# A Fourier mixing block on one core: the first batch's transposes on TensorE, its folds behind the inverse stage, and a new pacing of the seams

## The chip, the core and the metric

The kernel runs on one core of a Trainium2 chip. Its engines are TensorE (PE, matrix products into PSUM), VectorE (DVE), ScalarE (ACT), GpSimd (POOL) and SyncE (SP); here SP issues every DMA, from one queue, and 16 DMA engines carry them out. The metric is the device time of one execution in microseconds (us), the median of several runs.

## The reference

Eight batches of 3136 tokens with 256 channels go through a filter in the frequency domain, a two-dimensional Fourier mixing, and a channel MLP:

```python
X = np.fft.rfft(x, axis=1);  Y = X * (filt_r + 1j * filt_i)
x = np.fft.irfft(Y, n=3136, axis=1)
mixed = np.real(np.fft.fft(np.fft.fft(x, axis=1), axis=2))
u = x + mixed
un = (u - mean(u)) / sqrt(var(u) + 1e-6)          # over the 256 channels
out = u + maximum(un @ w_ch1, 0) @ w_ch2          # 256 -> 1024 -> 256
```

## The kernel before

All products are done in float16 with values split into a high and a low part, so most products come in three (high-high, high-low, low-high).

**Per batch, the way there** (`there`: `forward1`, or `first_forward1` for batch 0, then `forward2`). The 3136-point transform is split into 112 x 28. `forward1` loads x in seven tiles, finds the largest absolute value (`absmax`, DVE) for a power-of-two scale, does 14 pieces of the first stage (L386; L328 in batch 0) and writes each split piece `ast` to a DRAM buffer `d1`. `forward2` works in seven pieces `ch`: it loads `at` from `d1` (L411, which changes the layout), and for each of two channel halves `spectrum` does the second stage (L434 and L435), multiplies by the filters (DVE L440, L444; POOL L448, L449; in batch 0 some of this goes to DVE through `half`), splits the result into `y16` (ACT L453, then L454) and transposes `y16` into `z` with a transposing DMA (L459). `fold` (POOL L467 and L488, ACT L487) adds and subtracts the two channel halves and keeps the sums in the ring `eo`, from which the channel mixing is done later. `inverse1` (L495 to L497) does the first inverse stage two pieces behind, splits it into `bt` (ACT L499, DVE L500) and writes it to DRAM `d2`.

**The way back** (`inverse2`). It loads `b` from `d2` (L529), does the second inverse stage (L551), scales it on ACT (L558) and stores it in DRAM `dy`, in slots that hold a token and its mirror.

**Groups.** 12,544 slots are taken in 49 groups of 256. `fetch(g)` loads y, `prepare(g)` does the channel mixing from `eo` (L620), adds it (`add`, L630), normalizes (ACT L710), splits into `u16` (ACT L713, then DVE or POOL L715) and transposes into `ut` with a transposing DMA (L716). `first_product(g, f)` (L738) and `second_product(g, f)` (L767) are the MLP in eight f-steps a group; L776 adds and the result is stored.

**Weights** come as 64-bit floats in eight raw loads (`load_weights`, L810), are widened on DVE (`widen`, L787 to L793), bounded, scaled and split (`split_weights`, L850 to L852).

**What sets the order.** `there` and `back` are generators; one `yield` is one step. `advance(n)` runs steps of the way there, `give(n)` steps of the way back, and both are called from the main loop after every f-step `q` at a pace set by `RISE`, `EARLY`, `SOON`, `STEPS` and `BACK`; `bring` forces what a group needs. `weigh` issues work on the weights at given steps (`LOAD_AT`, `WIDEN_AT`, ...). Before the main loop batch 0 goes through all its steps, then groups 0 and 1 are prepared. A planner then orders each engine's instructions by its own estimates of time; `after(mark)` keeps an instruction behind the marked one on the same engine. `bufs` is how many buffers share a tag; the tag "big" (7 buffers) holds x, at, z and raw words, the tag "y" (4) holds the groups' y and widened weights.

Of the kernel before, what the change touches and what calls it, by code (L numbers as in the profile page):

```python
# [190 lines left out]
def _program(ctx, tc, nc, a, NB):  # L191
# [27 lines left out]
    s1 = cp.tile([112, 2, 112], F16, name="s1")  # L219
    s1f = cp.tile([112, 112], F32, name="s1f")  # L220
# [4 lines left out]
    ident = cp.tile([128, 128], F32, name="ident")  # L225
    ones = cp.tile([1, 128], F32, name="ones")
    eps = cp.tile([128, 1], F32, name="eps")
# [130 lines left out]
    def forward1(b, d1):  # L358
        xs = [xp.tile([112, 4, 256], F32, tag="big", name=f"x_{b}_{q}") for q in range(7)]
        m = tp.tile([112, 8], F32, tag="mx", name=f"mx_{b}")  # L360
        lag = 2 if b else 0
        for q in range(7 + lag):
            with after(("y", 1), ("un", 0)) if b == 1 else nullcontext():
                if q < 7:
                    nc.sync.dma_start(xs[q], a["x"][b, :, 4 * q : 4 * q + 4])
                if q >= lag:
                    with after("h"):
                        absmax(m[:, q - lag : q - lag + 1], xs[q - lag], AX.XY)
            if q < 7:
                yield  # L370
# [28 lines left out]
    def forward2(b, d1, d2):  # L399
# [21 lines left out]
        def spectrum(ch, hf):  # L421
            at = ats[ch]
            if hf == 0:
                yts[ch] = fp.tile([128, 2, 2, 4, 56], F32, tag="yt", name=f"yt_{b}_{ch}", bufs=2)
            yt = yts[ch]
# [21 lines left out]
            t2v = t2.rearrange("p r (j q) -> p r j q", j=4)  # L447
            half(b, hf == 1).tensor_tensor(yh[:, 0], yh[:, 0], t2v[:, 1], op=ALU.subtract)  # L448
            nc.gpsimd.tensor_tensor(yh[:, 1], yh[:, 1], t2v[:, 0], op=ALU.add)  # L449
# [7 lines left out]
            if hf == 0:  # L457
                zs[ch] = xp.tile([128, 8, 256], F16, tag="big", name=f"z_{b}_{ch}")
            marks["z", ch] = nc.sync.dma_start_transpose(  # L459
                zs[ch][:, :, 128 * hf : 128 * hf + 128], y16.rearrange("p j l q -> p (j l q)")  # L460
            ).ins

# [27 lines left out]
        def inverse1(ch, h):  # L490
            z = zs[ch][:112].rearrange("p (j l) c -> p j l c", l=2)[:, 2 * h : 2 * h + 2]
            j = 4 * ch + 2 * h
            p = bank(f"i1_{b}_{ch}_{h}")[:112].rearrange("p (j c) -> p j c", j=2)
            for i in range(2):
                nc.tensor.matmul(p[:, i], i1[:, j + i, 0], z[:, i, 0], start=True, stop=False)  # L495
                nc.tensor.matmul(p[:, i], i1[:, j + i, 0], z[:, i, 1], start=False, stop=False)  # L496
                nc.tensor.matmul(p[:, i], i1[:, j + i, 1], z[:, i, 0], start=False, stop=True)  # L497
            bt = fp.tile([112, 2, 2, 256], F16, tag="ast", name=f"bt_{b}_{ch}_{h}", bufs=4)
            nc.scalar.copy(bt[:, :, 0], p)  # L499
            nc.vector.tensor_tensor(bt[:, :, 1], p, bt[:, :, 0], op=ALU.subtract)  # L500
            nc.sync.dma_start(d2[:, j : j + 2], bt)

        far = 3
        for c in range(far):
            load(c)
        for _ in range(PAUSE):
            yield
        for c in range(9):
            work = [
                (c, spectrum, 0), (c, spectrum, 1), (c, fold, None), (c - 2, inverse1, 0), (c - 2, inverse1, 1),  # L510
            ]
            for ch, f, arg in work:
                if 0 <= ch < 7:
                    f(ch) if arg is None else f(ch, arg)
                    yield
            load(c + far)

    def inverse2(b, d2):
# [6 lines left out]
        def load(c):  # L525
            if c < 7:
                bts[c] = fp.tile([112, 4, 2, 256], F16, tag="b2", name=f"b2_{b}_{c}", bufs=2)
                with after("dy"):
                    marks["b", c] = nc.sync.dma_start(  # L529
                        bts[c].rearrange("p j h c -> p (j h) c"), d2v[:, 8 * c : 8 * c + 8]  # L530
                    ).ins

        def store(k, s, r, ys, c, j0):
            rows = dy[k, 224 * c : 224 * c + 224].rearrange("(j s q) c -> s q j c", j=4, s=2)
            marks["dy"] = nc.sync.dma_start(rows[s, :, j0], ys[r : r + 28, j0]).ins

        load(0)
        yield
        for c in range(14):
# [59 lines left out]
    def fetch(g):  # L599
        y = ys_of[g] = mp.tile([128, 2, 2, 256], F32, tag="y", name=f"y_{g}", bufs=4)  # L600
        for t, (g0, g1) in enumerate(groups[g]):
            q = g0
            while q < g1:
                b = q // NS
                e = min(g1, (b + 1) * NS)
                with after(("ut", 0)) if g == 2 else after(("out", g - 4)):
                    marks["y", g] = nc.sync.dma_start(
# [44 lines left out]
    def prepare(g):  # L652
# [52 lines left out]
        for t, (g0, g1) in enumerate(tiles):  # L705
# [9 lines left out]
            marks["u16", g] = low.tensor_tensor(u16[:m, :, :, 1], unv, u16[:m, :, :, 0], op=ALU.subtract).ins  # L715
            marks["ut", g] = nc.sync.dma_start_transpose(ut[:, t, :, :m], u16[:m].rearrange("p k d l q -> p (k d l q)")).ins  # L716
            yield
# [35 lines left out]
    def second_product(g, f):  # L753
# [8 lines left out]
        for t, (g0, g1) in enumerate(tiles):  # L762
# [12 lines left out]
            if f == 7:  # L775
                nc.vector.scalar_tensor_tensor(  # L776
                    y[:m, t], acc[:m], beta[:m], y[:m, t], op0=ALU.mult, op1=ALU.add
                )
                marks["out", g] = nc.sync.dma_start(a["out"][:, g0:g1].rearrange("k s c -> s k c"), y[:m, t]).ins

# [31 lines left out]
    def widen_weights(i):  # L812
# [54 lines left out]
    def advance(n):  # L867

        while done[0] < min(n, NB * STEPS):
            b, s = divmod(done[0], STEPS)  # L870
            if s in folds and b * NS + folds[s] - RING > mixed[0]:
                return
# [9 lines left out]
    folds = {20 + PAUSE + max(4 + 3 * ch, 5 * ch): 224 * ch + 224 for ch in range(7)}  # L882

    def need(slot):

        return BACK * (slot // NS) + 2 * (slot % NS // 224) + 3

    def bring(slot):
        advance(STEPS * (slot // NS + 1))
        give(need(slot))  # L890
# [47 lines left out]
    for q in range(8 * ng + LAG):  # L938
# [71 lines left out]
```

## Time and profile before

| | us |
|---|---|
| median of 3 runs | 1548.83 |
| range of the runs | 1542.42 to 1549.5 |
| profiled execution | 1553.5 |
| its span | 1551.7 |
| PE busy | 1403.2 (90% of the span) |
| DVE busy | 1095.7 (71%) |
| ACT busy | 757.2 (49%) |
| POOL busy | 535.7 (35%) |

Mean granted TensorE clock: 0.939 of full speed. The span runs from the first to the last instruction of one profiled execution; the profiled execution's own time is a little longer. A row of a group of instructions gives line, engine, operation, output from input, shapes and count, then busy us and mean ns of one, then the idle time before them and what ended it. A row of a timeline or of the chain gives start and duration in us. A row of the waits gives who waited for whom: us in total, times, longest. PE's durations in a row overlap (products are pipelined); the distance of their starts is what one costs.

### The profile page before, as it was taken

The numbers are of one execution on the slowest core, as the hardware profiler recorded it, in microseconds if no ns is written. First come the engines' busy times: TensorE is split into PE (matmuls) and PEld (weight loads), VectorE is DVE, ScalarE is ACT, GpSimd is POOL, SyncE is SP. The second block draws the span as 40 slices with busy tenths as digits, with TensorE's granted clock in tenths as the row PEclk, the third lists the DMA queues.
The fourth block names the chain that finished last, engine by engine and source line by source line (L and its number), as shares of the span: only waits on it lengthen the run. The fifth ranks groups of instructions, "written<-read, shape, count | busy, mean of one in ns | idle before, by whom it ended". The sixth has DMA issues, their size and how long they took to land.

```text
span 1551.7 us, 30099 instructions
## 1 busy us (share of the span) xinstructions
PE 1403.2 (90%) x11203; PEld 937.8 (60%) x11203; DVE 1095.7 (71%) x2395; ACT 757.2 (49%) x1409; POOL 535.7 (35%) x675
## 2 busy tenths in 40 slices
PE   5444998887999999999989899899999999999998
PEld 2431666554766667665766576665676666766666
DVE  5776877686768867786767777687857878565462
ACT  3256554364645545364535555364543755443431
POOL 3732038306710474006720175003740076110110
PEclk7565999998999999999999999999999999999999
DMA  8999269859983898559883799639994598644420
GB/s 251 221 277 254 67 157 204 192 168 207 214 230 98 229 217 219 135 151 216 202 213 83 192 211 206 187 107 200 219 220 122 165 223 192 170 110 122 106 52 31
DMA packets 446388, 273.17 MB, mean 176 GB/s; under 512 B 235521, under 2 KB 412721, under 8 KB 446241
## 3 DMA queue, kind: packets, MB, share of 16 engines
q1 hardware_dynamic: 446240, 271.25, 72.5%
q8 instruction: 88, 1.44, 0.4%
q14 instruction: 60, 0.48, 0.1%
HBM read 113.36 MB, written 102.76 MB: 139 GB/s over the span
## 4 chain that ended last, share of the span: by engine, by line
PE 67%; DMA 14%; DVE 8%; POOL 4%; issue 3%; ACT 2%; SPq 1%; DVEq 0%; ACTq 0%; POOLq 0%
PE h L738 27%; PE acc L767 26%; PE s L386 4%; PE y L551 3%; DMA d<-bt 3%; DMA at<-d 2%; PE mix L620 2%; DMA ut<-u 2%; DMA z<-y 2%; DMA d<-ast 2%; DMA x<-x 1%; DMA b<-d 1%; PE i L495 1%; DVE y L630 1%; PE i L496 1%
## 5 line engine op out<-in xcount | busy, mean ns | idle before, releaser
L738 PE MATMUL h<-ut,w1s 128*128 128x512 f16 x2352 | 594.4, 387 | 34.4 <-DMA ut<-u 28.9
L767 PE MATMUL acc<-w2s,h 128*128 128x256 f16 x4704 | 601.0, 274 | 3.9 <-ACT h L747 3.9
L767 PEld LDWEIGHTS <-h 128*128 128x128 f16 x4704 | 457.1, 98 | 152.5 <-issue 15.6
L748 DVE SCALAR_TENSOR_TENSOR h<-h,h 128x512 f16<-128x512 f32 x392 | 267.3, 684 | 238.2 <-ACT h L747 237.1
L747 ACT ACTIVATE h<-h 128x512 f16<-128x512 f32 x392 | 233.0, 594 | 369.9 <-PE h L738 363.6
L738 PEld LDWEIGHTS <-w1s 128*128 128x128 f16 x2352 | 225.3, 99 | 256.6 <-issue 44.4
L715 POOL TENSOR_TENSOR u<-un,u 128x512 f16<-128x512 f32 x94 | 107.8, 1163 | 730.1 <-ACT u L713 649.0
L630 DVE SCALAR_TENSOR_TENSOR y<-mix,alpha,y 128x508 f32<-128x508 f32 (+1 forms) x368 | 156.4, 474 | 10.2 <-DMA y<-dy 8.2
L558 ACT ACTIVATE ys<-y,alpha 128x512 f32<-128x512 f32 x112 | 75.8, 684 | 98.1 <-PE y L551 97.8
L710 ACT ACTIVATE un<-y,sb 128x256 f32<-128x256 f32 x196 | 101.7, 589 | 42.6 <-DVE sb L703 39.8
L454 POOL TENSOR_TENSOR y<-yt,y 128x448 f16<-128x448 f32 x105 | 108.5, 1037 | 28.5 <-ACT y L453 28.2
L551 PE MATMUL y<-b,i 112*64 112x512 f16 (+1 forms) x480 | 78.0, 419 | 37.4 <-DMA b<-d 28.3
L500 DVE TENSOR_TENSOR bt<-i,bt 112x512 f16<-112x512 f32 x112 | 75.7, 683 | 50.9 <-ACT bt L499 50.8
L448 POOL TENSOR_TENSOR yt<-yt,t 128x224 f32<-128x224 f32 x105 | 70.5, 671 | 115.3 <-DVE t L444 59.3
L440 DVE SCALAR_TENSOR_TENSOR yt<-s,pF,ft 128x448 f32<-128x448 f32 x112 | 75.6, 676 | 38.9 <-PE s L435 35.4
L499 ACT CAST bt<-i 112x512 f16<-112x512 f32 x112 | 65.0, 583 | 73.9 <-PE i L497 52.8
L453 ACT CAST y<-yt 128x448 f16<-128x448 f32 x112 | 62.5, 562 | 60.9 <-POOL yt L449 57.9
L776 DVE SCALAR_TENSOR_TENSOR y<-acc,beta,y 128x512 f32<-128x512 f32 x98 | 71.5, 745 | 23.8 <-PE acc L767 23.5
L434 PE MATMUL s<-s,at 112*128 112x56 f16 x896 | 65.5, 194 | 24.7 <-DMA at<-d 21.5
L495 PE MATMUL i<-z,i 112*112 112x256 f16 x224 | 64.7, 289 | 25.0 <-DMA z<-y 17.7
L386 PE MATMUL s<-x,s 112*112 112x512 f16 x294 | 85.9, 385 | 0.0
L389 DVE TENSOR_TENSOR ast<-s,ast 112x512 f16<-112x512 f32 x98 | 66.7, 681 | 24.0 <-ACT ast L388 23.7
(127 smaller groups left out, 1637.4 us busy)
## 6 DMA issues: line engine op xcount, KB each, us to landing
x<-x SPq DMA_DIRECT2D x56, 448.0 KB
d<-ast SPq DMA_DIRECT2D x112, 224.0 KB
at<-d SPq DMA_DIRECT2D x56, 448.0 KB
d<-bt SPq DMA_DIRECT2D x112, 224.0 KB
b<-d SPq DMA_DIRECT2D x56, 448.0 KB
out<-y SPq DMA_DIRECT2D x98, 256.0 KB
y<-dy SPq DMA_DIRECT2D x92, 256.0 KB
dy<-ys SPq DMA_DIRECT2D x208, 112.0 KB
```

The source lines that it names most:

```text
L386: nc.tensor.matmul(p, s1[:, hs], x16[:, hx], start=i == 0, stop=i == 2)
L454: last = half(b, hf == 1).tensor_tensor(ylo, ytv, yhi, op=ALU.subtract)
L495: nc.tensor.matmul(p[:, i], i1[:, j + i, 0], z[:, i, 0], start=True, stop=False)
L551: nc.tensor.matmul(p[64 * h : 64 * h + 64, js], i2[:, t, h, i], bt[:, o + js.start : o + js.stop, h], start=i == 0, stop=i == 1,)
L558: nc.scalar.activation(ys[:, o : o + 2], p, AF.Copy, scale=al[:, 2:3])
L630: nc.vector.scalar_tensor_tensor(out, p, al, y, op0=ALU.mult, op1=ALU.add)
L710: nc.scalar.activation(un[:m, k], y[:m, t, k], AF.Identity, bias=sb[:m, i, 1:2], scale=sb[:m, i, 3:4])
L715: marks["u16", g] = low.tensor_tensor(u16[:m, :, :, 1], unv, u16[:m, :, :, 0], op=ALU.subtract).ins
L738: marks["pe"] = nc.tensor.matmul(p[:, c0 : c0 + n].rearrange("p (t k q) -> p t k q", k=2, q=m), w1s[:, d, hw, 128 * f : 128 * f + 128], ut ...
L747: nc.scalar.activation(h[:, 0, :nt], p[:, :nt], AF.Relu)
L748: marks["h"] = nc.vector.scalar_tensor_tensor(h[:, 1, :nt], p[:, :nt], 0.0, h[:, 0, :nt], op0=ALU.max, op1=ALU.subtract).ins
L767: nc.tensor.matmul(acc[:m, k], h[:, hh, c0 : c0 + m], w2s[:, f, hw], start=f == 0 and k == 0 and i == 0, stop=f == 7 and k == 1 and i == 2,)
```

## The change

- `flip` transposes on TensorE: each 128-column block of a tile is transposed into one PSUM bank, and ACT copies the bank to its place. Batch 0 uses it for z in place of the transposing DMA (14 times), group 0 for ut (twice). A float16 identity `ident16` is made for it.
- In batch 0 the folds of pieces 2 to 6 are issued behind the last `inverse1`; their spectra are kept until then, four of them in the "y" buffers. In other batches a fold is issued after the inverse products of its step and one piece later. One subtraction of the second channel half in batch 0 (L448) goes from DVE to POOL.
- Four raw weight loads are issued during the last pieces of batch 0's first stage, four during its spectrum stage; widening stands behind the last `bt` subtraction.
- Pacing: absmax three steps behind its x load in place of two; x loads of batches from 2 on stand behind the last marked DMA; the three at loads are a step apart, and four steps lie between the first of them and the first spectrum, in place of two; two more empty steps between the first b load and its product; the way back is issued one step an f-step at most and begins 300 slots earlier; the last fold of a batch need not be done before its way back begins; `EARLY` is 0.6 in place of 0.54.

```diff
-PAUSE = 2
-STEPS = 22 + PAUSE + 7 * 5
-BACK = 15
-EARLY = 0.54
+PAUSE = 4
+XLAG = 3
+FIRST = 21 + XLAG
+STEPS = FIRST + PAUSE + 7 * 5
+WAIT = 2
+BACK = 1 + WAIT + 14
+EARLY = 0.6
+LOADED = 300
-LOAD_AT = (52, 52, 52, 52, 61, 61, 61, 61)
-LOAD_AFTER = (("z", 5), ("z", 5), ("z", 6), ("z", 6)) + (("b", 1),) * 4
-LOAD_IN = ('ut', 'ut', 'big', 'big', 'big', 'big', 'big', 'big')
-WIDEN_AT = (56, 57, 58, 59, 62, 63, 64, 65)
+LOAD_AT = (19, 20, 21, 22, 50, 50, 54, 54)
+LOAD_AFTER = (("d1", 10), ("d1", 11), ("d1", 12), ("d1", 13), ("bt", 3), ("bt", 3), ("bt", 4), ("bt", 4))
+LOAD_IN = ("ut", "ut", "ys", "ys", "big", "big", "big", "big")
+WIDEN_AT = (58, 59, 60, 61, 62, 63, 64, 65)
...
+    def flip(dst, src, pool, tag, name):
+        m, n, q = src.shape
+        pt = pool.tile([128, 8, 128], F16, tag=tag, name=name)
+        for i in range(n):
+            nc.tensor.transpose(pt[:q, i, :m], src[:, i], ident16[:m, :m])
+        return nc.scalar.copy(dst, pt[:q, :n, :m])
...
     # forward1
+                    with after("sp") if b > 1 else nullcontext():
+                        nc.sync.dma_start(xs[q], a["x"][b, :, 4 * q : 4 * q + 4])
...
     # spectrum
+                pool, tag, bufs = (mp, "y", 4) if b == 0 and 2 <= ch < 6 else (fp, "yt", 2)
...
-            half(b, hf == 1).tensor_tensor(yh[:, 0], yh[:, 0], t2v[:, 1], op=ALU.subtract)
+            nc.gpsimd.tensor_tensor(yh[:, 0], yh[:, 0], t2v[:, 1], op=ALU.subtract)
...
+            if b == 0:
+                marks["z", ch] = flip(
+                    z[:112], y16.rearrange("p j l q -> p (j l) q")[:, :, :112], ps_o, "pso", f"zt_{ch}_{hf}"
+                ).ins
+            else:
+                marks["z", ch] = nc.sync.dma_start_transpose(z, y16.rearrange("p j l q -> p (j l q)")).ins
...
     # forward2
         for c in range(far):
             load(c)
-        for _ in range(PAUSE):
+            if b:
+                yield
+        for _ in range(PAUSE - far if b else PAUSE + XLAG - 1):
             yield
...
-                (c, spectrum, 0), (c, spectrum, 1), (c, fold, None), (c - 2, inverse1, 0), (c - 2, inverse1, 1),
+                (c, spectrum, 0), (c, spectrum, 1), (c - 2, inverse1, 0), (c - 2, inverse1, 1),
+                (c - 1 if c < 7 else c - 2 if c == 8 else -1, fold, None),
...
-                if 0 <= ch < 7:
+                if 0 <= ch < 7 and (b or f is not fold or ch < 2):
...
+        for ch in range(2, 7) if b == 0 else ():
+            fold(ch)
+            yield
...
     # inverse2
         load(0)
-        yield
+        for _ in range(1 + WAIT):
+            yield
...
     # prepare
+            if g == 0:
+                ub = u16[:m].rearrange("p k d l q -> p (k d l) q")
+                flip(ut[:, t, :, :m], ub, ps_f, "psf", f"utt_{t}")
+            else:
...
     # widen_weights
-            with after("ylo" if "ylo" in marks else ("dve", 13)):
+            with after("low"):
...
     # give
-        while come[0] < min(n, NB * BACK) and done[0] >= STEPS * (come[0] // BACK + 1):
+        while come[0] < min(n, NB * BACK) and done[0] >= STEPS * (come[0] // BACK + 1) - 1:
...
+    def soon(slot):
+        return max(need(slot), BACK * ((slot + LOADED) // NS) + 1 + WAIT)
...
     # main loop
+        give(min(come[0] + 1, soon(32 * q + SOON)))
         advance(int(STEPS * (1 + min((q + 1) / RISE, (q + 1) / per + EARLY))))
-        give(BACK * (32 * q + SOON) // NS)
```

More of the change, by code (lines that the diff above doesn't have):

```diff
@@ L219, in _program @@
     s1 = cp.tile([112, 2, 112], F16, name="s1")
-    s1f = cp.tile([112, 112], F32, name="s1f")
+    s1f = fp.tile([112, 112], F32, tag="t2", name="s1f", bufs=2)
     s2 = cp.tile([112, 56, 2, 56], F16, name="s2")
@@ L225, in _program @@
     ident = cp.tile([128, 128], F32, name="ident")
+    ident16 = cp.tile([128, 128], F16, name="ident16")
     ones = cp.tile([1, 128], F32, name="ones")
@@ L235, in _program @@
     make_identity(nc, ident)
+    nc.scalar.copy(ident16, ident)
     nc.vector.memset(ones, 1.0)
@@ L360, in forward1 @@
         m = tp.tile([112, 8], F32, tag="mx", name=f"mx_{b}")
-        lag = 2 if b else 0
-        for q in range(7 + lag):
+        for q in range(7 + XLAG):
             with after(("y", 1), ("un", 0)) if b == 1 else nullcontext():
                 if q < 7:
-                    nc.sync.dma_start(xs[q], a["x"][b, :, 4 * q : 4 * q + 4])
-                if q >= lag:
+                    with after("sp") if b > 1 else nullcontext():
+                        nc.sync.dma_start(xs[q], a["x"][b, :, 4 * q : 4 * q + 4])
+                if q >= XLAG:
                     with after("h"):
-                        absmax(m[:, q - lag : q - lag + 1], xs[q - lag], AX.XY)
-            if q < 7:
+                        absmax(m[:, q - XLAG : q - XLAG + 1], xs[q - XLAG], AX.XY)
+            if q < 6 + XLAG:
                 yield
@@ L499, in inverse1 @@
             nc.scalar.copy(bt[:, :, 0], p)
-            nc.vector.tensor_tensor(bt[:, :, 1], p, bt[:, :, 0], op=ALU.subtract)
-            nc.sync.dma_start(d2[:, j : j + 2], bt)
+            marks["low"] = nc.vector.tensor_tensor(bt[:, :, 1], p, bt[:, :, 0], op=ALU.subtract).ins
+            marks["bt", ch] = nc.sync.dma_start(d2[:, j : j + 2], bt).ins
         far = 3
@@ L528, in load @@
                 with after("dy"):
[L529 removed]
+                    marks["b", c] = marks["sp"] = nc.sync.dma_start(
                         bts[c].rearrange("p j h c -> p (j h) c"), d2v[:, 8 * c : 8 * c + 8]
@@ L605, in fetch @@
                 e = min(g1, (b + 1) * NS)
-                with after(("ut", 0)) if g == 2 else after(("out", g - 4)):
+                with after(("un", 0)) if g == 2 else after(("out", g - 4)):
                     marks["y", g] = nc.sync.dma_start(
@@ L715, in prepare @@
             marks["u16", g] = low.tensor_tensor(u16[:m, :, :, 1], unv, u16[:m, :, :, 0], op=ALU.subtract).ins
-            marks["ut", g] = nc.sync.dma_start_transpose(ut[:, t, :, :m], u16[:m].rearrange("p k d l q -> p (k d l q)")).ins
+            if g == 0:
+                ub = u16[:m].rearrange("p k d l q -> p (k d l) q")
+                flip(ut[:, t, :, :m], ub, ps_f, "psf", f"utt_{t}")
+            else:
+                marks["sp"] = marks["ut", g] = nc.sync.dma_start_transpose(
+                    ut[:, t, :, :m], u16[:m].rearrange("p k d l q -> p (k d l q)")
+                ).ins
             yield
@@ L778, in second_product @@
                 )
-                marks["out", g] = nc.sync.dma_start(a["out"][:, g0:g1].rearrange("k s c -> s k c"), y[:m, t]).ins
+                marks["sp"] = marks["out", g] = nc.sync.dma_start(a["out"][:, g0:g1].rearrange("k s c -> s k c"), y[:m, t]).ins
     def widen(dst, raw, name):
@@ L870, in advance @@
             b, s = divmod(done[0], STEPS)
+            if s == 0 and come[0] < BACK * (b - 1) + 1:
+                return
             if s in folds and b * NS + folds[s] - RING > mixed[0]:
@@ L876, in give @@
     def give(n):
-        while come[0] < min(n, NB * BACK) and done[0] >= STEPS * (come[0] // BACK + 1):
+        while come[0] < min(n, NB * BACK) and done[0] >= STEPS * (come[0] // BACK + 1) - 1:
             next(home)
             come[0] += 1
-    folds = {20 + PAUSE + max(4 + 3 * ch, 5 * ch): 224 * ch + 224 for ch in range(7)}
+    folds = {FIRST + PAUSE + (4, 9, 14, 19, 24, 29, 34)[ch]: 224 * ch + 224 for ch in range(7)}
     def need(slot):
-        return BACK * (slot // NS) + 2 * (slot % NS // 224) + 3
+        return BACK * (slot // NS) + 1 + WAIT + 2 + 2 * (slot % NS // 224)
+    def soon(slot):
+        return max(need(slot), BACK * ((slot + LOADED) // NS) + 1 + WAIT)
     def bring(slot):
-        advance(STEPS * (slot // NS + 1))
+        advance(STEPS * (slot // NS + 1) - 1)
         give(need(slot))
```

14 lines of the change are left out of this document (6 added, 8 removed).

## The prediction

> **What bounds the kernel now.** I read the page first, then the span cut into stages, then 5 us slices of the first stage, the groups of instructions, the chain that ended last, and the waits of TensorE (PE). The stages (busy us of PE, PE weight loads, DVE, ACT, POOL with counts, granted clock, DMA share, GB/s):
>
> ```profile
> 0.00:149.80 149.80, 68.20 (x453) 43.16 (x453) 101.95 (x215) 68.17 (x132) 65.65 (x85) 0.62 0.93 252
> 149.80:400.00 250.20, 220.75 (x1796) 145.41 (x1797) 190.51 (x400) 125.54 (x233) 96.36 (x125) 0.94 0.74 170
> 400.00:1300.00 900.00, 867.12 (x7114) 581.89 (x7113) 669.46 (x1468) 465.90 (x867) 339.75 (x430) 0.98 0.78 185
> 1300.00:1551.70 251.70, 247.16 (x1844) 167.37 (x1842) 133.81 (x315) 97.61 (x179) 33.98 (x36) 1.00 0.41 103
> ```
>
> There are two programs in one. Up to 149.8 us, when the first product of the channel MLP starts, PE is busy 68.2 us and everything waits for batch 0 to come through. From then on PE is busy 1335.0 of 1401.9 us, so the end is set by PE's work plus its 66.9 us idle. Hence: time = start of the first product + 1335 + what PE idles. An edit counts if it moves the first product or removes PE idle time. The profiled execution took 1553.5 us (1.8 more than its span); the median of the runs is 1548.83, 4.7 lower. I work out differences in the span and take them off the median. About 0.5% (7.7 us) is what a measurement of this kernel can tell from no change.
>
> **Start-up, first half: the spectrum stage of batch 0 (45.7 to 102.5 us).**
>
> ```profile
> 25.00:30.00 5.00, 3.08 (x5) 0.93 (x4) 2.58 (x5) 4.97 (x11) 4.83 (x5) 0.50 0.58 201
> 35.00:40.00 5.00, 1.84 (x6) 0.55 (x4) 3.31 (x12) 2.70 (x7) 0.05 (x1) 1.00 0.51 155
> 55.00:60.00 5.00, 2.78 (x12) 2.40 (x12) 4.88 (x10) 2.37 (x5) 4.79 (x7) 0.50 0.94 231
> 65.00:70.00 5.00, 2.28 (x35) 1.74 (x33) 4.42 (x8) 2.08 (x4) 5.00 (x8) 0.50 1.21 266
> 70.00:75.00 5.00, 4.27 (x44) 4.10 (x44) 3.57 (x7) 2.23 (x5) 4.58 (x6) 0.50 1.13 323
> 45.71 0.23 PE L434 MATMUL s<-s,at 112*128 112x56 f16 x1 [6.11 <-DMA at<-d]
> 45.76 0.23 PE L435 MATMUL s<-s,at 112*128 112x56 f16 x1
> 81.41 0.25 PE L434 MATMUL s<-s,at 112*128 112x56 f16 x1
> L448 POOL TENSOR_TENSOR yt<-yt,t 128x224 f32<-128x224 f32 x105 | 70.5, 671 | 115.3 <-DVE t L444 59.3
> L467 POOL TENSOR_TENSOR ef<-yt 128x224 f32<-128x224 f32 x112 | 73.8, 677 | 0.8
> L488 POOL TENSOR_TENSOR eo<-ef,eo 128x448 f16<-128x448 f32 (+6 forms) x62 | 58.9, 953 | 35.4 <-ACT eo L487 34.7 <-DMA ut<-u 0.7
> L454 POOL TENSOR_TENSOR y<-yt,y 128x448 f16<-128x448 f32 x105 | 108.5, 1037 | 28.5 <-ACT y L453 28.2
> L453 ACT CAST y<-yt 128x448 f16<-128x448 f32 x112 | 62.5, 562 | 60.9 <-POOL yt L449 57.9
> L280 ACT ACTIVATE squares<-ft 128x784 bf16<-128x784 f32 x4 | 3.4, 849 | 0.0
> 56.85 0.43 PE L495 MATMUL i<-z,i 112*112 112x256 f16 x1 [3.58 <-DVE yt L440]
> 57.08 0.42 PE L496 MATMUL i<-z,i 112*112 112x256 f16 x1
> 111.10 1.37 PE L620 MATMUL mix<-mix,eo 128*128 128x129 f16 x13
> ```
>
> In the slices from 55 us the fifth busy number, POOL, is 4.6 to 5.0 of 5 us, and DMA's share is about 1: POOL sets the pace, DMA is full beside it. A piece (one of seven) costs POOL one L448 (0.67), two L449 (0.67 each, the same form as L448), one L454 (1.04), two L467 (0.68 each) and one L488 (0.95): 5.4 us; the measured period is (81.41 - 45.71)/6 = 5.95.
>
> *Folds moved back* (the "sums for the mixing"). Pieces 2 to 6 lose L467 x2 and L488 here, and gain the second L448, which goes from DVE to POOL: 4 x 0.67 + 1.04 = 3.7 us. POOL is no longer the bound. The five folds then run on POOL behind the last spectrum, about 4 us each with one buffer: 20 us. Their results are wanted by the second group only; the first group takes pieces 0 and 1, whose folds stay. Four of the "y" buffers hold the kept spectra, so the first fetch of y waits for fold 4, some 12 us behind the last spectrum; the fetch comes about 30 us behind it. Cost nothing, covered by the inverse stage.
>
> *z by TensorE.* Removed: 14 DMA transposes from SP's queue and the DMA engines. Added: 8 transposes of 112 or 128 columns and one ACT copy of 1024 columns for each half. A transpose streams 128 columns through PE; the nearest row is L620 at the same half clock, 1.37/13 = 0.105 us, so 0.84 us for eight. The ACT copy: L280 with 784 columns takes 0.849, L453 with 448 takes 0.562; the line through them gives 1.05 us at 1024. New loads per piece: ACT 2 x 0.56 + 2 x 0.58 + 2 x 1.05 = 4.4 (the 0.58 is L499 below); PE at half clock 32 x 0.047 (45.76 - 45.71) + 12 x 0.22 (57.08 - 56.85) + 1.7 = 5.8. So the period lies between 4.4 (ACT) and 5.95 (nothing won); I take 5.2, nearer PE's number, because the clock column stands at 0.50 in the three slices from 55 us, with PE up to 85% busy. 6 x 0.75 = 4.5 us. The Trainium skill (TensorE: Matmul & The Clock Gate, Part 1: The HAM clock gate) says that about 3.4 us of sustained work lifts PE from half to full clock; the slice 70 to 75, 4.27 us busy at 0.50, does not bear that out by itself. If it held here, ACT's 4.4 would be the period and the term 4.8 us larger.
>
> ```profile
> L499 ACT CAST bt<-i 112x512 f16<-112x512 f32 x112 | 65.0, 583 | 73.9 <-PE i L497 52.8 <-DMA d<-bt 12.1 <-issue 4.8
> L500 DVE TENSOR_TENSOR bt<-i,bt 112x512 f16<-112x512 f32 x112 | 75.7, 683 | 50.9 <-ACT bt L499 50.8
> 100.28 2.25 DMA d<-bt
> 102.69 0.92 SPq L529 DMA_DIRECT2D b<-d  x2
> 107.11 1.92 PE L551 MATMUL y<-b,i 112*64 112x256 f16 x12 [8.94 <-DMA b<-d]
> 104.31 6.87 DMA raw<-w
> 111.19 3.54 DMA dy<-ys
> 114.74 1.92 ACT w L850 x3
> 123.84 0.73 DVE y L630
> 135.37 2.08 ACT L710 ACTIVATE un<-y,sb 128x256 f32<-128x256 f32 x4 [0.81 <-DVE sb L703]
> 137.35 1.12 ACT L713 CAST u<-un 128x512 f16<-128x512 f32 x2
> 141.54 8.21 DMA ut<-u
> 149.80 0.61 PE h L738
> ```
>
> Tail of the stage: last spectrum at 81.41 to the last d2 landing at 102.53 is 21.1 us. After: products 1.5, four DVE steps 2.7 at most, POOL 1.3, ACT 0.6, DVE 0.8, flip 1.9, twelve inverse products 2.6, bt 1.3, landing 2.25, hand-overs 0.6: 15.5. Gain 5.6 us.
>
> *Weights loaded earlier.* Four of the eight raw loads (512 KB each) go in SP's queue behind the last four d1 writes, ahead of the first at load. 2.1 MB at the stage's 252 GB/s is 8.3 us of DMA in a place where the engines were half idle (share 0.58 and 0.51 in the first two slices); at can be late by 0 to 4 us, I take 2. So the first half wins 4.5 + 5.6 - 2 = 8.1 us.
>
> **Start-up, second half (102.5 to 149.8).** The chain shows four raw loads (6.87 us) between the loads of b and the dy stores, then weight scaling on ACT (1.92). All raws are now ahead of this stage. b's load (4.4 us from issue to the first product at 107.11) runs in part beside the raws, so of the 8.8 us I take 5. From 123.84 to 135.37 DVE works four widening instructions into the chain, some 0.5 each; they now stand behind the last bt subtraction and are mostly done: gain 2.
>
> *First ut by TensorE.* 135.37 to 149.80 is 14.4 us, 8.21 of it the transposing DMA. After: un 2.08, u16 1.12, DVE 0.7, PE 0.84, two ACT copies 2.1: 6.8. Gain 7.6. Only group 0; group 1 keeps its DMA, covered by eight f-steps of group 0. The Trainium skill (VectorE: DVE Perf Modes, The three transpose paths) gives 390 ns for a 128x128 transpose on TensorE; eight in a row would be 3.1 us, and by it the sum would be about 7 us smaller.
>
> Sum: 8.1 + 5 + 2 + 7.6 = 22.7 us, first product near 127. Bounds: 4 (period unchanged, tail 3, at 4 late, and little of the rest) to 34 (period 4.4, no delay, raws fully off the path). One ident16 copy and s1f's new buffer cost nothing: ACT and "t2" idle then.
>
> **Seams between batches.** What PE waited for after 155 us (total, times, longest):
>
> ```profile
> PE h L738 <- DMA ut<-u: 16.8, 4, 12.3
> PE s L434 <- DMA at<-d: 14.3, 10, 2.9
> PE y L551 <- DMA b<-d: 13.9, 5, 4.1
> PE i L495 <- DMA z<-y: 5.3, 5, 2.7
> 287.21 10.18 DMA x<-x
> ```
>
> at and b together are 28.2 us: the loads are issued one or two steps before PE wants them. The change spaces the three at loads by a step and gives four steps in place of two; b gets three steps in place of one, and at most one step of the way back is issued in each f-step. An f-step lasts 1401.9/394 = 3.56 us, so both leads grow by about 7 us against waits of at most 4.1. I take two thirds: 19 us. Next in line is the ut wait (12.3 us at once), which this change touches only through the pacing. x loads of batches from 2 on are tied behind the last issued DMA in SP, so that they no longer block z and bt writes (10.18 us on the chain); absmax one step later. Against it, five more steps a batch and a larger lead for forward work squeeze POOL and DVE. I set these at -1 together; seams 18 us. From both sides: 38 (at, b and most of ut) and -8 (one new 12.3 us wait, 4 won).
>
> Total 22.7 + 18 = 40.7: 1548.8 - 40.7 = 1508.
>
> **Rivals.**
> 1. *The seams are only re-dealt.* Instructions are put in order before the run by estimated times; new waits of 2 to 4 us replace the old. For: the 12.3 us wait has no edit that names its cause. Against: 28 us stand in two kinds of wait with a plain cure. 1548.8 - 22.7 = 1526.
> 2. *PE at half clock bounds the spectrum stage*, flips in PE's in-order queue wait for ACT and hold the next spectra. For: clock 0.50 and 5.8 us of work a piece. Against: in the slice from 65 us PE was busy only 2.28 of 5 us, so it was not PE that the stage waited for. Start-up wins about 8, with the seams 26: 1523.
> 3. *Slower: the way back comes late.* One step an f-step and two more empty steps put y's fetch 2 x 3.56 = 7.1 us later at each of seven seams, and the first product of a new batch waits for it. 7 x 7.1 = 50 against 22.7: +27, 1576. It decides from 22.7/7 = 3.2 us a seam. Against: a fetch that is due still forces all steps before it, and loads start 300 slots earlier.
> 4. *Given back.* An earlier first product only means that batch 1 is awaited sooner: 1541 to 1549. For: the stage from 149.8 to 400, in which batch 1 first has to deliver, is the one with most idle, 29.5 us. Against: its steps are issued by f-steps, that is by PE's own progress.
>
> **How the numbers follow.** Forecast 0.52, rivals 0.20, 0.13, 0.07, 0.08. Faster by over 0.5% (below 1541): 0.52 + 0.20 + 0.13 = 0.85; within: 0.08; slower: 0.07. The forecast's own range is 1490 to 1525. The range given, 1486 to 1534, takes in rivals 1 and 2 and the bounds: 1548.8 - 34 - 28 at the best, 1548.8 - 4 - 11 at the worst.
>
> **What would show it.** First product of L738 near 127 us (right between 120 and 135). POOL under 4 of 5 us and spectrum products about 5.2 us apart in the stage; at's first products near 47.5. No raw load between b and dy. From un to the first product under 8 us. at and b waits of PE under 10 us together after the start. I am wrong if the first product comes after 140, if PE's idle time behind it stays at 60 us or more, or if PE's busy time behind it is not near 1335.

## The result and the profile after

The changed kernel takes 1536.39 us (median of seven runs, 1535.45 to 1543.25) against 1548.83 us (median of seven; 1542.42 to 1551.23). The ratio is 0.9941, 95% interval 0.9921 to 0.9961: faster by 0.6%, 12.4 us of the 40.7 forecast. The profiled execution after took 1535.8 us, span 1534.0; against the span before (1551.7) that is 17.7 us less, 5 more than the medians differ by. So the stages below, which are of these two executions, show some 5 us more gain than the kernel has.

The span of the changed kernel in the same four stages (columns as before the change):

```profile
0.00:147.40 147.40, 70.91 (x584) 46.13 (x584) 90.93 (x190) 78.80 (x143) 70.43 (x92) 0.70 0.81 224
147.40:400.00 252.60, 222.16 (x1810) 145.81 (x1809) 195.40 (x415) 126.54 (x236) 97.93 (x129) 0.94 0.74 176
400.00:1300.00 900.00, 876.08 (x7257) 588.16 (x7257) 688.21 (x1504) 477.95 (x886) 350.06 (x442) 0.99 0.80 189
1300.00:1534.00 234.00, 229.55 (x1684) 153.95 (x1681) 118.30 (x282) 88.05 (x162) 21.48 (x19) 1.00 0.38 93
```

The first product of the channel MLP starts at 147.4 in place of 149.8: the start gave 2.4 us of 22.7. From there to the end it is 1386.6 us in place of 1401.9: 15.3 us of the 18 put on the seams. But PE's idle time fell by only 8.1 of these (66.9 to 58.8); PE's busy time fell by the other 7.2 (1335.0 to 1327.8), which the forecast held constant.

The start in the changed kernel's timeline, in order. New line numbers: L449 spectra, L519 last step of the inverse stage, L577 b's products, L633 fetch of y, L656 add, L819 widening of the weights, L866 the weights' bounds, L882 scaling of the weights, L884 their split on POOL, L736 un, L739 u16, L274 flips, L275 copies out of PSUM, L646 the next group's channel mixing, L770 the first product:

```profile
49.17 0.23 PE L449 MATMUL s<-s,at 112*128 112x56 f16 x1 [9.36 <-DMA at<-d]
78.46 0.19 PE L449 MATMUL s<-s,at 112*128 112x56 f16 x1
95.34 0.69 DVE L519 TENSOR_TENSOR bt<-i,bt 112x512 f16<-112x512 f32 x1 [0.59 <-ACT bt L518]
95.95 0.42 DVE L819 TENSOR_SCALAR cv<-raw 128x512 int32<-128x512 int32 x1
97.29 0.69 DVE L821 SCALAR_TENSOR_TENSOR w<-raw,w 128x512 int32<-128x512 int32 x1
102.92 3.62 PE L577 MATMUL y<-b,i 112*64 112x256 f16 x20 [8.28 <-DMA b<-d]
118.69 0.91 SPq L633 DMA_DIRECT2D y<-dy  x2
122.32 5.57 POOL L884 TENSOR_TENSOR w1s<-w,w1s 128x512 f16<-128x512 f32 x4 [18.45 <-ACT w1s L883]
122.38 1.38 DVE L819 TENSOR_SCALAR cv<-raw 128x512 int32<-128x512 int32 x1
125.35 1.53 DVE L821 SCALAR_TENSOR_TENSOR w<-raw,w 128x512 int32<-128x512 int32 x1
126.80 2.43 DVE L656 SCALAR_TENSOR_TENSOR y<-mix,alpha,y 128x508 f32<-128x508 f32 x5
132.43 0.37 PE L250 MATMUL pt_w<-ident,mw 128*1 128x128 f32 x1 [10.39 <-ACT mw L866]
134.99 2.07 ACT L736 ACTIVATE un<-y,sb 128x256 f32<-128x256 f32 x4 [1.05 <-DVE sb L729]
136.97 2.54 ACT L882 ACTIVATE w<-w,sw 128x512 f32<-128x512 f32 x4
139.42 1.12 ACT L739 CAST u<-un 128x512 f16<-128x512 f32 x2
142.50 1.67 PE L274 MATMUL utt<-ident,u 128*128 128x128 f16 x14
143.68 1.90 ACT L275 COPY ut<-utt 128x1024 f16<-128x1024 f16 x2
143.97 3.00 PE L646 MATMUL mix<-mix,eo 128*128 128x129 f16 x32
146.89 0.62 PE L577 MATMUL y<-b,i 112*64 112x512 f16 x4
147.45 0.82 PE L770 MATMUL h<-ut,w1s 128*128 128x512 f16 x3
```

b's first product comes 4.2 us earlier than before (102.92 against 107.11), so the spectrum stage did win something. From there to the first product it is 44.5 us, where before it was 149.80 - 107.11 = 42.7: the second half of the start, which was to win 14.6 us, lost 1.8. The reader should see what stands in it. The widening begins at 95.95, right behind the last step of the inverse stage, and its last pieces (steps of 1.38 to 1.53 us while POOL splits w1) hold DVE up to the add at 126.80. The add also needs y, whose fetch SP issues at 118.69, behind a dy store and 15.8 us behind b's first product. The second weight's bounds go through PE at 132.43, and its scaling (2.54 us on ACT) stands between un and u16. The copies of ut end at 145.6, but PE then has the next group's mixing and four of b's products ahead of the first product.

What PE waited for behind its first product, and DVE's wait for x (total, times, longest). In the trace of before the last stood at 4.7 us:

```profile
PE h L770 <- DVE h L780: 20.5, 12, 4.1
PE s L449 <- DMA at<-d: 17.6, 10, 10.4
PE h L770 <- DMA ut<-u: 4.1, 2, 3.2
PE y L577 <- DMA b<-d: 2.7, 3, 1.9
DVE mx L267 <- DMA x<-x: 43.8, 21, 5.4
```

b's wait is cured (13.9 to 2.7), at's is not (14.3 to 17.6), ut's fell (16.8 to 4.1). Of at's 17.6 one wait is 10.4. A new one, PE waiting for DVE's half of the hidden layer, stands at 20.5 (5.5 before), and DVE itself stands 43.8 us in front of x loads that have not landed.

### The profile page after: what moved, and what is told of

It is laid out like the page before. It is cut to its first block, busy times and chain, and to the rows that moved or that the text cites. A ratio compares the mean times of both kernels' runs of the same rounds, so it can differ in the third digit from the quotient of the medians.

```text
span 1534.0 us, 30300 instructions
## 1 busy us (share of the span) xinstructions
PE 1398.7 (91%) x11331; PEld 934.1 (61%) x11331; DVE 1092.8 (71%) x2388; ACT 771.3 (50%) x1426; POOL 539.9 (35%) x682
## 4 chain that ended last, share of the span: by engine, by line
PE 67%; DMA 11%; DVE 7%; issue 3%; POOL 3%; ACT 2%; SPq 1%; DVEq 0%; POOLq 0%; ACTq 0%
PE h L770 26%; PE acc L799 26%; DMA x<-x 3%; PE s L400 3%; PE y L577 3%; DMA at<-d 2%; PE mix L646 2%; DVE y L656 2%; PE i L514 1%; DMA b<-d 1%; PE i L516 1%; PE i L515 1%; PE s L449 1%; DVE mx L267 1%; PE s L450 1%
## 5 line engine op out<-in xcount | busy, mean ns | idle before, releaser
L770 PE MATMUL h<-ut,w1s 128*128 128x512 f16 x2352 | 590.8, 385 | 24.6 <-DVE h L780 20.5
L799 PEld LDWEIGHTS <-h 128*128 128x128 f16 x4704 | 456.4, 98 | 146.8 <-issue 13.6
L770 PEld LDWEIGHTS <-w1s 128*128 128x128 f16 x2352 | 223.8, 99 | 236.7 <-issue 48.1
L656 DVE SCALAR_TENSOR_TENSOR y<-mix,alpha,y 128x508 f32<-128x508 f32 (+1 forms) x368 | 156.0, 474 | 8.2 <-PE mix L646 6.9
L736 ACT ACTIVATE un<-y,sb 128x256 f32<-128x256 f32 x196 | 101.8, 589 | 44.0 <-DVE sb L729 38.8
L519 DVE TENSOR_TENSOR bt<-i,bt 112x512 f16<-112x512 f32 x112 | 75.7, 682 | 49.1 <-ACT bt L518 47.4
L267 DVE TENSOR_REDUCE mx<-x 112x1 f32<-112x1024 f32 x56 | 67.7, 1214 | 52.0 <-DMA x<-x 52.0
L463 POOL TENSOR_TENSOR yt<-yt,t 128x224 f32<-128x224 f32 x112 | 73.9, 660 | 81.9 <-DVE t L459 53.6
L449 PE MATMUL s<-s,at 112*128 112x56 f16 x896 | 62.7, 191 | 32.6 <-DMA at<-d 28.1
L577 PE MATMUL y<-b,i 112*64 112x512 f16 (+1 forms) x480 | 74.1, 396 | 18.1 <-DMA b<-d 17.9
L808 DVE SCALAR_TENSOR_TENSOR y<-acc,beta,y 128x512 f32<-128x512 f32 x98 | 71.2, 742 | 25.7 <-PE acc L799 25.5
L449 PEld LDWEIGHTS <-at 112*128 112x128 f16 x896 | 55.8, 98 | 42.6 <-DMA at<-d 36.0
```

Source lines behind the costliest of these rows:

```text
L449: nc.tensor.matmul(o, w, s2[:, U, 0].rearrange("p (r k) -> p r k", r=2), start=True, stop=False)
L577: nc.tensor.matmul(p[64 * h : 64 * h + 64, js], i2[:, t, h, i], bt[:, o + js.start : o + js.stop, h], start=i == 0, stop=i == 1,)
L656: nc.vector.scalar_tensor_tensor(out, p, al, y, op0=ALU.mult, op1=ALU.add)
L736: nc.scalar.activation(un[:m, k], y[:m, t, k], AF.Identity, bias=sb[:m, i, 1:2], scale=sb[:m, i, 3:4])
L770: marks["pe"] = nc.tensor.matmul(p[:, c0 : c0 + n].rearrange("p (t k q) -> p t k q", k=2, q=m), w1s[:, d, hw, 128 * f : 128 * f + 128], ut ...
L799: nc.tensor.matmul(acc[:m, k], h[:, hh, c0 : c0 + m], w2s[:, f, hw], start=f == 0 and k == 0 and i == 0, stop=f == 7 and k == 1 and i == 2,)
```

## The experiments

Four questions: does the start lose its gain to the weights' work, or do the flips not deliver; is a gain at the start kept behind it; do the seams' edits or the start's edits give the 15.3 us; is the new wait for DVE caused by the tied x loads. Ratios are to the kernel before, with 95% intervals; spans and stages are of one profiled execution each, which can lie 6 to 9 us from the median of its kernel (z_dma 1544.5 against 1550.5, folds_late 1542.8 against 1534.1).

### The two halves apart

**seams_only**: the changed pacing with the first batch as before (flips, folds, weights' places undone). **start_only**: the changed first batch with the old pacing (PAUSE 2, XLAG 2, WAIT 0, EARLY 0.54, x loads not tied, `give` as before). Both keep the folds of the later batches one piece later.

> The changed kernel's pacing between batches with the first batch as it was before (z and the first ut by transposing DMA, folds in place, raw weights loaded late). Prediction's seam term (18 us): first product near 150 us, as before, and about 1531 to 1536 us. If the two parts need each other: clearly over 1540. In the traces the first product moved 2.4 us and the rest of the span shrank by 15; if that split is real this kernel should be at about 1537.

> The changed kernel's first batch with the pacing of before. If the start is worth what its first product shows (2.4 us), 1545 to 1548 us. If the start was worth the predicted 22.7 us and the changed pacing spoils it, first product near 127 and about 1527 us.

seams_only: 1550.27 us, ratio 1.0018 (1.0000 to 1.0037). start_only: 1542.86 us, 0.9969 (0.9944 to 0.9994). Alone, the pacing gains nothing and the start 0.3%. The table at the end of this section has their stages: both halves change what PE waits for, but neither the 2.4 nor the 15.3 us belongs to one edit alone.

### The start: the flips

```
 z_dma:   -            if b == 0:            ut_dma:  -            if g == 0:
          +            if False:                      +            if False:
          (z of batch 0 by DMA again)                 (ut of group 0 by DMA again)
```

> The changed kernel with z of batch 0 transposed by DMA again, ut of group 0 still by TensorE. By the prediction's working the flips save some 3 us behind the last spectrum and free the DMA engines: first product of b 3 to 6 us later than 102.8, the MLP 3 to 6 us later than 147.4, 1538 to 1542. If the folds alone carried the stage's gain: within 2 us in both.

> The changed kernel with ut of group 0 transposed by DMA again, z still by TensorE. The time from normalization to the first product was 14.4 us before and is 12.5 now. If the flip itself is worth the predicted 7.6 us and only the w2 split ate it: 18 to 20 us here, first product 153 to 155. If DMA would do as well now that x loads come earlier: 12 to 14.5, first product within 2 us of 147.4, time within 3 us of 1536.

z_dma: 1550.48 us, 1.0008 (0.9990 to 1.0027), 14.1 us above the changed kernel. PE's waits up to 115 us in it, and b's first product:

```profile
PE i L514 <- DMA z<-y: 18.3, 4, 6.1
111.01 3.20 PE L577 MATMUL y<-b,i 112*64 112x256 f16 x18 [8.31 <-DMA b<-d]
```

b's first product is 8.1 us later (102.92 to 111.01) and the first product of the MLP 8.2 us (155.6). The flips of z deliver: 8.1 us at b, of the 10.1 (4.5 + 5.6) that the forecast gave to flips and folds together. The other 6 us by which the median is longer aren't in this execution: behind its first product it takes 1387.1 us, as the changed kernel does (1386.6).

ut_dma: 1543.42 us, 0.9967 (0.9944 to 0.9990). Its first product stands at 148.4, only 0.9 us later. Un starts at 135.16 (134.99 with the flip); the transposing DMA is issued at 141.58 and the first product follows 6.8 us later, 13.2 us behind un. With the flip the last 14 transposes start at 142.50 and the product follows 5.0 us later, 12.5 us behind un. The term of 7.6 us was worth 0.9: what stands between un and u16 stands there with either, and behind the flips PE does the next group's mixing and b's products (143.97 to 147.5) before the first product, while in ut_dma it has done them by 132.3 and waits 13.6 us for ut.

### The start: the weights' work

```
 one_copy    -                widen(w, words[i], f"{i}")
             +                nc.vector.tensor_copy(w, words[i].bitcast(F32)[:, :, 1])
 early_w1    -WIDEN_AT = (58, 59, 60, 61, 62, ...    -BOUND_AT = (62, 66)    -SPLIT_AT = (63, 115)
             +WIDEN_AT = (23, 24, 25, 26, 62, ...    +BOUND_AT = (27, 66)    +SPLIT_AT = (58, 115)
 no_weights  widening, bounds, scaling and splits left out; memset weights and beta
```

> The changed kernel with the widening of the weights (four DVE and one ACT instruction a piece) cut to one DVE copy of the high words, so that the weights' values are other numbers; everything else is there. Theory W (the weights' chain from 96 to 146 us holds the start): first product 6 to 12 us earlier than 147.4, time 1525 to 1531. Theory Q (the order in SP's queue holds it: at of piece 4 behind the first bt write, y of group 0 behind the dy stores of pieces 2 and 3): first product within 3 us, time 1533 or more.

> The changed kernel with the first weight matrix widened and bounded right behind its loads, in DVE's idle time from 40 to 50 us, and split one step earlier. Theory W: first product 4 to 8 us earlier, time 1528 to 1533. Theory Q: the planner's order of SP changes too here (at of piece 4 comes ahead of the first bt write, y of group 0 right behind the dy stores of piece 1), so it also expects a gain, by the spectrum stage ending about 5 us earlier and y landing 5 us earlier; the two are told apart by where the time goes: W sees add start earlier at an unchanged landing of y, Q the landing of y itself.

> The changed kernel without the work on the weights: the raw words are loaded, but widening, bounding and splitting are left out, and both weight tiles are filled with a constant at the start. If the prediction's sum for the start fails through the weights' chain alone: first product near 127 to 131. If the rest of the sum is wrong as well: one_copy took 9.5 us off by most of this work, so 134 to 138.

one_copy: 1529.3 us, 0.9879 (0.9843 to 0.9916); first product 137.9. early_w1: 1531.35 us, 0.9892 (0.9853 to 0.9932); first product 142.8, although its b stage begins 7.6 us later (110.6), since the split of w1 then stands on POOL among the spectra. no_weights (two runs): 1529.86 us, 0.9885 (0.9816 to 0.9955); rows of its timeline, with line numbers three higher:

```profile
102.55 3.62 PE L580 MATMUL y<-b,i 112*64 112x256 f16 x20 [8.32 <-DMA b<-d]
109.57 0.52 SPq L636 DMA_DIRECT2D y<-dy  x1
...
113.74 1.79 DVE L659 SCALAR_TENSOR_TENSOR y<-mix,alpha,y 128x508 f32<-128x508 f32 x4 [14.23 <-ACT keep L700]
...
127.97 1.67 PE L277 MATMUL utt<-ident,u 128*128 128x128 f16 x14
...
132.42 1.90 PE L773 MATMUL h<-ut,w1s 128*128 128x512 f16 x8
```

Nothing moved up to b (102.55 against 102.92), and from there it is 29.9 us in place of 44.5: leaving out the weights' work brings 14.6 us, all of it between b and the first product. The fetch of y goes out 9 us earlier and the add 13 us earlier; 3.0 of the 14.6 lie behind un (12.5 to 9.5 us to the first product). In one_copy the same stretch is 137.94 - 104.48 = 33.5 us: shortening the widening alone, on DVE (four instructions a piece to one) and on ACT (one to none), brings back 11.0 of the 14.6.

How the work costs this much is only in part shown. The planner orders SP's queue anew as well, and in all three kernels it puts y's first fetch ahead of dy stores that stand ahead of it in the changed kernel. In one_copy:

```profile
111.43 0.51 SPq L633 DMA_DIRECT2D y<-dy  x1
```

That is 7.0 us behind b's first product (104.48), 7.0 in no_weights and 7.6 in early_w1, against 15.8 in the changed kernel. So the expectation's theory Q, SP's order, is not ruled out beside theory W: up to 9 us of the stretch can be this order, which the planner chose with the weights' work in its estimates. No run moves the fetch alone.

### The start: smaller suspects

**folds_late** holds folds 2 to 6 on POOL until the last spectrum is through (`with after("pool"): fold(ch)`), because in the changed kernel the planner ran two of them inside the stage. **w2_late** puts the second weight's split behind the flips of u (`after(("un", 0), "utc")`). **far4** lets four at loads run ahead in batch 0 (`far = 3 if b else 4`). **combo_a** has the first weight early, four loads ahead, dy stores behind y's fetch, and w2_late's edit.

> The changed kernel with the folds of pieces 2 to 6 held behind the last y16 subtraction on POOL; in the changed kernel POOL runs two of them inside the spectrum stage. Theory F (they keep the last pieces back): last bt write 3 to 5 us earlier, first product of b near 99, the MLP's first product 2 to 4 us earlier at most, since the weights' work (theory W) starts behind the last bt and moves with it; time 1532 to 1536. If POOL was not what the last piece waited for: first product of b unchanged at 102.8.

> The changed kernel with the scaling and splitting of the second weight matrix put behind the two copies of the first ut on ACT. From the normalization to the first product it took 12.5 us where 6.8 was predicted; ACT works 4.7 us on w2 in between. If that is the reason: 12.5 falls to 7 to 9, the first product to about 143. Rival: the second product needs w2 and waits for it, so that the time stays at 1535 to 1538 whatever the first product does; a gain over 3 us speaks against that.

> The changed kernel with four at loads ahead in batch 0 in place of three, so that at of piece 4 stands ahead of the first bt write in SP's queue. Theory Q: PE's 9.4 us wait for at goes, the first product of b comes 4 to 8 us before 102.8, the first MLP product about 140 to 143, time 1528 to 1532. Theory W: b's first product comes earlier as well, but the weights' work behind the last bt keeps its length, so the MLP starts at 145 or later and the time stays within 1533 to 1538.

> Four edits to the changed kernel together: w1 widened in DVE's idle time from 40 to 50 us (split where it was), four at loads ahead, stores of pieces 2 and later of batch 0 behind the first fetch of y, w2's split behind the first ut. Theory W and Q together: first product 130 to 137, time 1520 to 1528. If what one edit frees is taken by the next wait: first product not under 140.

folds_late: 1534.13 us, 0.9918 (0.9892 to 0.9944); b's first product at 103.8, no earlier. The folds are not what the last piece waited for. w2_late: 1541.48 us, 0.9939 (0.9915 to 0.9963). It brings the first product to 145.4, 9.0 us behind un in place of 12.5, but the stretch behind is 7.7 us longer. The split of w2 now ends at 151.8 us in place of 145.7, and the second layer of the MLP needs it, but no wait of PE for it stands in the trace; the cause stays open. far4: 1529.02 us, 0.9874 (0.9821 to 0.9926), with the start unchanged (first product 147.0); its whole gain lies behind the first product, where it changes nothing by itself. The order of the instructions is planned anew for every edit, and with nothing else changed behind the start the time there is 9.0 us less (the medians differ by 7.4). So a difference of that size behind the start can't be put down to an edit unless a wait in the trace names it. combo_a: 1534.82 us, 0.9905 (0.9871 to 0.9938); first product 140.25, behind it 7.2 us more than in the changed kernel, much as with w2_late.

### The seams

```
 x_free        -                    with after("sp") if b > 1 else nullcontext():
               (x loads in SP's queue as before the change)
 xlag5, xlag7  -XLAG = 3
               +XLAG = 5   (7)      absmax five (seven) steps behind its x load; weights' places moved along
```

> The changed kernel with the x loads of batches from 2 on free in SP's order, as before (not tied behind the last marked DMA). Theory D (the tie makes x late, DVE stands in absmax, and PE waits for the split of h behind it): DVE's wait for x loads after the start falls from 43.8 us to under 10, PE's wait for DVE's h from 20.5 to under 9, time 1524 to 1530. Rival: x loads block SP again, PE's wait for ut returns from 4 to over 10 us, and the time stays within 4 us of 1536.

> The changed kernel with absmax five steps behind its x load in place of three, x loads still tied in SP. Theory D (the tie lets b go first but makes DVE stand in absmax until x is there): DVE's wait for x falls from 43.8 us to under 15, PE's wait for DVE's h from 20.5 to under 9, b waits stay under 6, time 1526 to 1531. If the waits move on: another wait of PE grows by as much, time 1533 or more.

> The changed kernel with absmax seven steps behind its x load. Theory D: DVE's wait for x falls from 16.9 (lag 5) to under 6, PE's wait for DVE's h from 8.5 to under 5, time 1519 to 1523. Rival: what is left are waits for at, ut and z (28 us with lag 5), which a longer way there only makes worse: 1523 to 1530.

x_free: 1540.33 us, 0.9926 (0.9895 to 0.9957): no gain. PE's waits behind its first product and DVE's for x:

```profile
PE y L576 <- DMA b<-d: 25.1, 7, 6.8
PE s L448 <- DMA at<-d: 14.0, 10, 4.1
PE h L769 <- DVE h L779: 2.0, 3, 1.2
DVE mx L267 <- DMA x<-x: 2.9, 4, 1.0
```

With the tie gone DVE no longer stands (43.8 to 2.9) and PE no longer waits for DVE (20.5 to 2.0). b's wait comes in its place (2.7 to 25.1). So the larger lead of b does not cure its wait without the tie of the x loads (whether the tie would without the lead, no run shows); the price is the wait for DVE. xlag5 keeps the tie and asks for x later: 1523.91 us, 0.9851 (0.9814 to 0.9888), with x5_wide (below) the fastest of all kernels here. Its waits:

```profile
PE s L449 <- DMA at<-d: 13.4, 12, 2.3
PE h L770 <- DMA ut<-u: 10.8, 2, 8.3
PE h L770 <- DVE h L780: 8.3, 10, 2.8
PE y L577 <- DMA b<-d: 2.0, 4, 0.7
DVE mx L267 <- DMA x<-x: 16.9, 11, 5.8
```

DVE's wait falls to 16.9, PE's for DVE to 8.3, and b stays cured. xlag7 takes DVE's wait down further, to 8.7, but not PE's for it (7.9), and has 1540.2 us, 0.9935 (0.9908 to 0.9961): the lead of five is not improved by seven. Most of the 18.2 us by which it falls behind xlag5 from the first product on are slower products (1333.8 busy against 1322.9) at a lower clock (below), the rest idle time in many small waits. Since the waits for b and DVE are as short in xlag7 and the time is not, the 12.5 us of xlag5 aren't shown to be those waits' alone.

### Both repairs together

**x5_early**: xlag5 and early_w1's places. **x5_wide**: xlag5, the first weight widened early and the folds late.

> absmax five steps behind its x load (xlag5, 1523.9 us) together with the first weight matrix widened early and split at the folds (early_w1, first product at 142.8). If a gain at the start adds to a gain at the seams: 1518 to 1521 us, 1373 to 1376 us behind the first product. If batch 1 then comes too late and the start is given back: 1523 to 1526.

> xlag5 with the first weight matrix widened early, split where it was, and the folds of pieces 2 to 6 held behind the spectrum stage. Additive: first product 140 to 143, time 1516 to 1521. Given back: first product earlier and 1523 or more.

x5_early: 1530.34 us, 0.9885 (0.9834 to 0.9935). x5_wide: 1524.22 us, 0.9856 (0.9802 to 0.9910). Their first products come 6.0 and 7.7 us earlier than xlag5's and the time behind is 7.0 and 7.2 us longer: here, as far as one execution each can tell, the gain at the start was given back, a small part of it in a ut wait (longest 12.2 and 10.7 us, 8.3 in xlag5).

The stages of the profiled executions, us (idle is the stretch behind the first product less PE's busy time in it; clock is the mean granted there):

| | first product | behind it | PE busy | PE idle | clock | waits at / b / ut / DVE h |
|---|---|---|---|---|---|---|
| before | 149.8 | 1401.9 | 1335.0 | 66.9 | 0.97 | 14.3 / 13.9 / 16.8 / 5.5 |
| after | 147.4 | 1386.6 | 1327.8 | 58.8 | 0.98 | 17.6 / 2.7 / 4.1 / 20.5 |
| seams_only | 152.6 | 1398.8 | 1333.8 | 65.0 | 0.97 | 19.0 / 2.2 / 3.4 / 17.7 |
| start_only | 147.1 | 1392.9 | 1328.9 | 64.0 | 0.98 | 12.1 / 18.1 / 9.6 / 6.3 |
| one_copy | 137.9 | 1388.9 | 1326.5 | 62.4 | 0.98 | 17.8 / 3.6 / 3.3 / 17.5 |
| no_weights | 132.4 | 1393.2 | 1331.5 | 61.7 | 0.98 | 15.0 / 4.5 / 2.6 / 22.4 |
| far4 | 147.0 | 1377.6 | 1321.6 | 56.0 | 0.99 | 15.7 / 2.4 / 3.2 / 19.1 |
| x_free | 147.4 | 1391.3 | 1330.1 | 61.2 | 0.98 | 14.0 / 25.1 / 7.1 / 2.0 |
| xlag5 | 147.9 | 1373.0 | 1322.9 | 50.1 | 0.99 | 13.4 / 2.0 / 10.8 / 8.3 |
| xlag7 | 148.3 | 1391.2 | 1333.8 | 57.4 | 0.98 | 14.7 / 2.6 / 11.3 / 7.9 |

## Why the prediction was wrong

**The step that failed is the second half of the start**: "All raws are now ahead of this stage ... I take 5", of the widening "they now stand behind the last bt subtraction and are mostly done: gain 2", and "First ut by TensorE ... Gain 7.6". Together 14.6 us were forecast and -1.8 came. Without the weights' work the stretch from b to the first product is 29.9 us; the forecast had 42.7 - 14.6 = 28.1. The sum was about right for a kernel whose weights are ready, though not its last term: from un to the first product it is 9.5 us there, and 6.8 were forecast, without PE's other work that stands behind the flips. The weights were not ready: only the loads were moved ahead of the stage. The widening was tied behind the last bt subtraction, where it starts later (95.95 against 90.61) than in the kernel before and ends little earlier (129.82 against 131.25), and with the bounds, the scaling and the splits it stands on DVE and ACT between b and u. The forecast costed the tie as a gain at one place and never listed what the tied work needs: 4.2 us a piece for eight pieces (95.95 to 129.82). How much of the loss is these engines and how much the later fetch of y that came with them stays open.

**The first half** was to win 8.1 us and won 4.2 at b. Its terms: the period went from 5.95 to (78.46 - 49.17)/6 = 4.9, 6.4 us and not 4.5; at was 3.5 us late (49.17 against 45.71), not 2; the tail to the last landing was 20.2 us (98.63 - 78.46), not 15.5, and this is the term that was mis-sized. In the trace its chain goes through z copies, inverse products and bt casts of the last two pieces, one behind the other (82.28 to 95.34), where the forecast counted one piece; no run tests this. The folds do not hold the tail, by folds_late.

With z_dma the flips are shown to be worth 8 us. "POOL under 4 of 5 us" was wrong: from 55 to 90 us it stayed at 4.6 to 5.0, with folds in the stage. These are 5 us slices of the changed kernel:

```profile
55.00:60.00 5.00, 3.63 (x49) 3.46 (x50) 3.40 (x12) 1.48 (x2) 4.62 (x8) 0.50 0.73 161
65.00:70.00 5.00, 3.76 (x64) 3.36 (x61) 4.47 (x8) 5.00 (x8) 4.86 (x7) 1.00 0.95 252
70.00:75.00 5.00, 3.31 (x72) 3.12 (x73) 4.27 (x8) 3.90 (x8) 4.83 (x6) 1.00 1.12 299
80.00:85.00 5.00, 2.38 (x29) 2.17 (x26) 3.97 (x7) 4.45 (x8) 4.74 (x7) 1.00 0.74 209
```

Rival 2, PE at half clock as the bound, is refuted: from 65 to 90 us the clock stands at 1.00, and in the slice at 0.50 PE is busy 3.63 of 5 us.

**The seams**: 18 forecast, 15.3 measured (10 by the medians), but not for the reason given, so that the nearness is in part luck: PE's idle time, out of which the 18 were to come, fell by 8.1. "b gets three steps in place of one" did not cure b by itself (x_free has the same steps and 25.1 us of b wait); the tied x loads were needed. at's waits did not fall in total (14.3 to 17.6). The tie was costed as part of "-1 together"; it made DVE stand 43.8 us and PE 20.5 for it. That PE's busy time stays at 1335 was wrong too: of the 15.3 us 7.2 are busy time.

**The rivals.** "The seams are only re-dealt" holds in part: new waits stand in place of the old (PE's for DVE, one of 10.4 us for at), and seams_only gains nothing, but together with the start's edits the stretch is 15.3 us shorter. "The way back comes late" (1576) is refuted: behind the first product none of PE's longer waits is for y's fetch. "Given back" is not what took the start's gain here: it was never there at the first product. With the changed pacing, one_copy keeps 9.5 - 2.3 = 7.2 us of what it wins at the start, early_w1 4.6 - 1.5 = 3.1; no_weights keeps 8.4 of 15.0; with xlag5's pacing nearly nothing is kept.

## What to carry to other kernels

Moving a load earlier wins nothing while the work on what it loads stays tied to a later event: list, for every load that is moved, who consumes it, on which engine, and between which two links of the critical chain that work then stands. Of a tie that keeps one kind of transfer out of another's way, ask which engine asks for the tied data next, and move that request along (XLAG 3 to 5: PE's wait for DVE from 20.5 to 8.3 us). Where a planner orders the instructions anew for each edit, a single edit can move distant stages by 7 to 9 us (far4), so read which wait changed and not only the total.

## What the runs showed of the hardware

**A wait costs PE more than its length.** A product of the kernel before with the wait ahead of it, and the 5 us slices around it:

```profile
994.70 1.92 PE L551 MATMUL y<-b,i 112*64 112x256 f16 x12 [4.12 <-DMA b<-d]
```

```profile
985.00:990.00 5.00, 5.00 (x37) 3.43 (x36) 4.96 (x11) 1.33 (x3) 0.00 (x0) 1.00 0.73 271
990.00:995.00 5.00, 0.88 (x10) 0.68 (x9) 5.00 (x11) 0.00 (x0) 0.00 (x0) 0.88 0.76 168
995.00:1000.00 5.00, 5.00 (x23) 2.29 (x20) 0.27 (x2) 1.97 (x3) 0.00 (x0) 0.50 0.40 97
1000.00:1005.00 5.00, 5.00 (x33) 3.25 (x32) 3.67 (x7) 0.79 (x2) 0.00 (x0) 0.94 0.53 144
```

After 4.12 us of waiting the clock stands at 0.50 for the next 5 us, with PE busy all the time. The Trainium skill (TensorE: Matmul & The Clock Gate, HAM oscillation — how this bites in real kernels) says that idle gaps longer than about 3.4 us throttle the clock again; this row agrees. Shorter waits went with it too: in xlag5, behind waits of 0.32 and 2.32 us between 690 and 695 us, the clock stood at 0.55 from 695 to 700. Summed over the 5 us slices from 160 us on, (1 - clock) x 5 us comes to 34.1 us before, 32.5 in seams_only, 28.9 in xlag7, 25.5 in start_only, 23.8 after, 17.7 in xlag5 and 15.4 in far4, and PE's busy time falls along it, 1335.0, 1333.8, 1333.8, 1328.9, 1327.8, 1322.9, 1321.6. No run changed the clock alone, so that the busy time follows from the clock is read from these seven and not shown by an experiment; nor is it strict (25.6 us went with 1331.1 in folds_late).

**DVE slows beside POOL.** The widening's step L821 of 128x512 takes 0.69 us (97.29 above), but 1.53 (125.35) while POOL splits w1 (122.32 to 127.89). The Trainium skill (GPSIMD Engine Reference, 8. Key points) says that the two share their SBUF interfaces and contend where a DVE instruction has two SBUF inputs, as this one has, or runs in a 2-port perf mode; the rows agree. The step L819, with one input, slows as well (0.42 at 95.95, 1.38 at 122.38); whether it runs in such a mode, no run shows.
